# Output projection of a linear-attention block: a fifth Strassen unit, part of its input sums on GpSimd, and another order of the units

## The chip, the cores and the metric

The kernel runs on one core of one Trainium2 chip. A core has five engines that run side by side, each with its own instruction queue: TensorE (PE, matmuls; its weight loads appear as PEld), VectorE (DVE), ScalarE (ACT), GpSimd (POOL) and SyncE (SP), which here issues most DMAs. They wait for each other through semaphores. Matmuls write into PSUM, eight banks of 128 x 512 fp32 values; everything else lies in SBUF. The metric is the device time of one execution in microseconds.

## The reference

```python
def _A_ref(x, wqkv, wo):
    qkv = ... (x @ wqkv) split into q, k, v of 32 heads of 32
    phi = lambda t: jnp.where(t > 0, t + 1, jnp.exp(t)) + 1e-6
    pq, pk = phi(q), phi(k)
    kv = jnp.einsum("bhsd,bhse->bhde", pk, v)
    z = jnp.einsum("bhsd->bhd", pk)
    num = jnp.einsum("bhqd,bhde->bhqe", pq, kv)
    den = jnp.einsum("bhqd,bhd->bhq", pq, z)[..., None] + 1e-6
    return (num / den) as (S, D) @ wo

def _B_ref(x, w_gate, w_up, w_down):
    return (silu(x @ w_gate) * (x @ w_up)) @ w_down

xn = layernorm(x)
out = x + _A_ref(xn, wqkv, wo) * silu(_B_ref(xn, w_gate, w_up, w_down))
```

x has 2048 rows of 1024, the feed-forward width is 3584, inputs are bfloat16. The change touches the last product of `_A_ref`, (num / den) @ wo.

## The kernel before

The 2048 rows are four blocks (b = 0 to 3) of 512, each of four tiles (t) of 128 rows. The kernel has three stages.

Stage one computes K and V and sums kv and z over all rows. Stage two takes the blocks in turn. `emit_Q` (L178) computes the Q product of one of eight groups g in a PSUM bank, and `emit_phi` (L145) applies phi: with `act=True` three ScalarE passes and one VectorE pass, which is put off (`phi_late`); with `in_place=True` and `act=False` one ScalarE pass (Exp) and two VectorE passes (L157, L163). `emit_ND` (L725, "nd" below) makes numerator and denominator of one tile and divides on VectorE; `emit_OT` (L753) transposes the result by a DMA from the SP queue into oT, the left operand of the output projection. oT has two buffers, so block 3 writes the one that block 1 used. `emit_S` (L758) is the direct projection: for one tile and one half of the columns, eight matmuls and one scaled copy on ScalarE; a ScalarE-issued DMA then stores the tile to `s_dram`. Stage three is the feed-forward part, from L940 on, which starts from sums of the normalized input made by `emit_Ssum` (L696, four VectorE sums S1 to S4 of 128 x 2048).

The last tiles of the projection are done by Strassen units (`s_unit`, L785): two tiles t1 and t2 and both column halves form a 2 x 2 by 2 x 2 block product, which takes seven products of four matmuls where the direct way takes 32 matmuls. A unit works in these steps, each an entry of a dictionary:

- sums: four sums so1, so2, so3 and S4 of 128 x 512 from the two oT tiles (L801 to L804, VectorE). S4 is written over part of the oT tile.
- x: product into bank X; ScalarE copies X into bank Y (L814).
- w: product of so1 into W; ScalarE makes w1 from W (L821).
- y: product of so2 added onto Y; ScalarE copies Y into bank Z (L826) and makes s2 from Y (L827).
- x2: product added onto X; ScalarE writes a result quarter (L831).
- z: product of so3 added onto Z; VectorE adds w1 and writes a quarter (L835, a scalar_tensor_tensor, "STT" below).
- z2: product added onto Z; ScalarE writes a quarter (L840); SP stores the tile.
- w2: product of S4 added onto W; VectorE adds s2 and writes a quarter (L845); SP stores the other tile.

The right operands of w, y, z and z2 are four sums of wo (To_sb), made once by GpSimd (L780). The kernel before has four units, two for block 2 and two for block 3; blocks 0 and 1 are direct. All of TensorE, VectorE, ScalarE, GpSimd and SP's queue stand in program order here, so the order of calls is the order of execution on each engine. The five banks are fx0 to fx4. s2 and e_t of `emit_phi` share two buffers (tag e_t); w1 has two (tag r_t).

Beside this, `prep_step` (L352) prepares weights for stage three: a load, a ScalarE pass of squares (L288), a power of two, a VectorE scaling (L311), four GpSimd sums (L323 to L326) and a store. Some of it runs inside `nd_item` (L860). Stage three's first weight loads wait for the x product of the unit that holds tile 0 of block 3 (`first_gate`, marks[("S", 3, 0)]).

Of the kernel before, what the change touches and what calls it, by code (L numbers as in the profile page):

```python
# [10 lines left out]
ALU = mybir.AluOpType  # L11
# [10 lines left out]
def kernel(  # L22
# [155 lines left out]
    def emit_Q(b, g, act=None):  # L178
        pqT = pqT_of(b)
        btok = slice(b * TB, (b + 1) * TB)  # L180
        q_ps = ps2.tile([P, TB], FP32, name="q_ps", tag="B2")
        for dc in range(DC):
            nc.tensor.matmul(q_ps[:], lhsT=wq_sb[:, dc, g * P:(g + 1) * P], rhs=xn_ap(dc, btok),  # L183
                             start=(dc == 0), stop=(dc == DC - 1))
        emit_phi(phiw, q_ps[:], pqT[:, g, :], TB, in_place=True, act=b > 0 if act is None else act)
# [528 lines left out]
    with ExitStack() as p2:  # L714
# [43 lines left out]
        def emit_S(b, t, cc, bank=None):  # L758
            oT = oT_tiles[b]
            ttok = slice(t * P, (t + 1) * P)  # L760
            if (b, t) not in s_tiles:
                s_tiles[(b, t)] = work.tile([P, D], BF16, name="s_sb", tag="s_sb")
            s_sb = s_tiles[(b, t)]
            s_ps = bank or ps2.tile([P, CW], FP32, name="s_ps", tag="B2")
            for c in range(G):
                mm = nc.tensor.matmul(s_ps[:], lhsT=oT[:, c, ttok], rhs=wo_sb[:, c, cc * CW:(cc + 1) * CW],  # L766
                                      start=(c == 0), stop=(c == G - 1))
                marks.setdefault(("S", b, t), mm)
            nc.scalar.activation(out=s_sb[:, cc * CW:(cc + 1) * CW], in_=s_ps[:], func=ACT.Copy, scale=s_sc[:])
            if cc == NCC - 1:  # L770
                r0 = b * TB + t * P
                nc.scalar.dma_start(out=s_dram[r0:r0 + P, :], in_=s_tiles.pop((b, t))[:])
# [9 lines left out]
        fx = []  # L782
        unit_n = [0]

        def s_unit(b, u):  # L785
            n = unit_n[0]
            unit_n[0] += 1
            oT = oT_tiles[b]
            t1, t2 = u, u + 2
            k1, k2_ = slice(t1 * P, (t1 + 1) * P), slice(t2 * P, (t2 + 1) * P)  # L790
            a11, a12 = oT[:, 0:HG, k1], oT[:, HG:G, k1]
            a21, a22 = oT[:, 0:HG, k2_], oT[:, HG:G, k2_]
            b11, b21, b22 = wo_sb[:, 0:HG, 0:CW], wo_sb[:, HG:G, 0:CW], wo_sb[:, HG:G, CW:D]
            X, Y, Z, W = fx[n % 2], fx[1 - n % 2], fx[2], fx[3 + n % 2]
            so = wq_sb[:, TPB:DC, :].rearrange("p a b -> p (a b)")[:, (n % 2) * 2048:(n % 2) * 2048 + 3 * HG * P]
            so = so.bitcast(F16).rearrange("p (q k t) -> p q k t", q=3, k=HG)
            S4 = a21.bitcast(F16)
            sb = {}

            def sums():  # L800
                nc.vector.tensor_tensor(out=so[:, 0], in0=a21, in1=a22, op=ALU.add)  # L801
                nc.vector.tensor_tensor(out=so[:, 1], in0=so[:, 0], in1=a11, op=ALU.subtract)
                nc.vector.tensor_tensor(out=so[:, 2], in0=a11, in1=a21, op=ALU.subtract)
                nc.vector.tensor_tensor(out=S4, in0=a12, in1=so[:, 1], op=ALU.subtract)  # L804

            def mmk(out, a_, b_, first):
                for k in range(HG):
                    mm = nc.tensor.matmul(out[:], lhsT=a_[:, k, :], rhs=b_[:, k, :], start=first and k == 0,  # L808
                                          stop=k == HG - 1, skip_group_check=True)
                return mm  # L810

            def x():
                marks[("S", b, u)] = mmk(X, a11, b11, True)
                nc.scalar.copy(out=Y[:], in_=X[:])  # L814

            def w():
                for t in (t1, t2):
                    s_tiles[(b, t)] = work.tile([P, D], BF16, name="s_sb", tag="s_sb")
                mmk(W, so[:, 0], To[0], True)
                sb["w"] = phiw.tile([P, CW], FP32, name="w1", tag="r_t")  # L820
                nc.scalar.activation(out=sb["w"][:], in_=W[:], func=ACT.Copy, scale=s_sc[:])  # L821

            def y():
                mmk(Y, so[:, 1], To[1], False)
                s2 = sb["s2"] = phiw.tile([P, CW], FP32, name="s2", tag="e_t")
                nc.scalar.copy(out=Z[:], in_=Y[:])  # L826
                nc.scalar.activation(out=s2[:], in_=Y[:], func=ACT.Copy, scale=s_sc[:])  # L827

            def x2():
                mmk(X, a12, b21, False)  # L830
                nc.scalar.activation(out=s_tiles[(b, t1)][:, 0:CW], in_=X[:], func=ACT.Copy, scale=s_sc[:])  # L831

            def z():
                mmk(Z, so[:, 2], To[2], False)
                nc.vector.scalar_tensor_tensor(out=s_tiles[(b, t2)][:, CW:D], in0=Z[:], scalar=s_sc[:],  # L835
                                               in1=sb["w"][:], op0=ALU.mult, op1=ALU.add)

            def z2():
                mmk(Z, a22, To[3], False)
                nc.scalar.activation(out=s_tiles[(b, t2)][:, 0:CW], in_=Z[:], func=ACT.Copy, scale=s_sc[:])  # L840
                out_s(b, t2)

            def w2():
                mmk(W, S4, b22, False)
                nc.vector.scalar_tensor_tensor(out=s_tiles[(b, t1)][:, CW:D], in0=W[:], scalar=s_sc[:],  # L845
                                               in1=sb["s2"][:], op0=ALU.mult, op1=ALU.add)
                out_s(b, t1)
            return dict(sums=sums, x=x, w=w, y=y, x2=x2, z=z, z2=z2, w2=w2)

        def out_s(b, t):  # L850
            r0 = b * TB + t * P
            nc.sync.dma_start(out=s_dram[r0:r0 + P, :], in_=s_tiles.pop((b, t))[:])

        def q_item(b, g):
            return lambda: emit_Q(b, g)

        def s_item(b, t, cc):
            return lambda: emit_S(b, t, cc)
# [15 lines left out]
        def mix(a, b_):  # L874
            r = []
            for k in range(max(len(a), len(b_))):
                r += a[k:k + 1] + b_[k:k + 1]
            return r

        def sh(b, hf):  # L880
            return [s_item(b, t, cc) for t in (2 * hf, 2 * hf + 1) for cc in range(NCC)]

        def run(body, at, b, order=(0, 1, 2, 3)):
            for k, f in enumerate(body):
                f()
                if k in at:
                    nd_item(b, order[at.index(k)])()
                phi_flush()

        def qs(b):  # L890
            return [q_item(b, g) for g in range(G)]

        run(qs(1), (1, 3, 5, 7), 0)
        q = qs(2)
        run(q[:2] + mix(q[2:], sh(0, 0) + sh(0, 1)), (1, 4, 7, 10), 1)
        q = qs(3)
        run(q[:2] + mix(q[2:], sh(1, 0)), (1, 4, 7, 10), 2, (0, 2, 1, 3))
        nds = [nd_item(3, t) for t in (0, 2, 1, 3)]
        emit_S(1, 2, 0)
        emit_S(1, 2, 1)  # L900
        fx.extend([ps2.tile([P, CW], FP32, name="fx%d" % k, tag="B2") for k in range(5)])
        units = [s_unit(2, 0), s_unit(2, 1)]
        u = units[0]
        nds[0]()
        u["x"]()
        u["sums"]()
        emit_S(1, 3, 0, fx[4])
        nds[1]()
        emit_S(1, 3, 1, fx[2])
        u["w"]()  # L910
        units[1]["sums"]()
        u["y"]()
        u["x2"]()
        nds[2]()
        u["z"]()
        parts = []
        for n in range(1, 4):
            u, v = units[n - 1], units[n]
            for st in ('x w nd new -z2 sums y -w2 x2 z', 'x w new Ssum -z2 sums p y -w2 x2 z p', 'x w -z2 y p -w2 z x2 p z2 silu w2')[n - 1].split():
                if st == "nd":  # L920
                    nds[3]()
                elif st == "new":
                    units.append(s_unit(3, n - 1))
                elif st == "sums":
                    units[n + 1]["sums"]()
                elif st == "p":
                    parts.pop(0)()
                elif st == "silu":
                    nc.scalar.preload_act_table(ACT.Silu)
                elif st == "Ssum":  # L930
                    blk_es.close()
                    blk12_es.close()
                    sp = ctx.enter_context(tc.tile_pool(name="p3S", bufs=1, side="right", reuse_waits="tile"))
                    emit_Ssum(passes[0], parts)
                    stat_ps[0] = lambda: psa_tile("st_ps3")[0][:, 0, 511:512]
                    prep_flush()
                elif st[0] == "-":
                    u[st[1:]]()
                else:
                    v[st]()  # L940
    p2_man.close()
    p12.close()

# [987 lines left out]
```

## Time and profile before

| what | us |
|---|---|
| runs before | 750.99, 751.78, 752.26 (median 751.78) |
| the profiled execution, its own time | 751.34 |
| span from its first to its last instruction | 749.6 |
| DMA, mean rate | 259 GB/s |

Line 1 of the page has each engine's busy time, its share of the span and its number of instructions; part 4 has the chain of work that ended last. A row of the order of time has the start in us from the span's start, the length, the engine, the line, the operation, what it writes and reads, and how many instructions were merged; in brackets the idle time before it and what ended it. A row of merged matmuls lasts until the last one's modelled end, so the next row starts 0.16 us before the former ends when TensorE runs without a gap. The granted TensorE clock is 1.000 over the span. The units of stage two stand between 214.5 and 244.3 us:

```profile
L808 PE MATMUL fx<-wo_sb,oT x48: 377/379/380, 214.5 to 244.1; 128*128 128x512 bf16 x48
L814 ACT COPY fx<-fx x4: 570/570/570, 215.6 to 237.4; 128x512 f32<-128x512 f32 x4
L826 ACT COPY fx<-fx x4: 570/570/570, 221.2 to 240.0; 128x512 f32<-128x512 f32 x4
L827 ACT ACTIVATE s<-fx,s_sc x4: 692/692/692, 221.7 to 240.5; 128x512 f32<-128x512 f32 x4
```

### The profile page before, as it was taken

The page shows a single profiled execution, that of the slowest core. Times are in us where ns is not written, and L with a number is a line of the kernel's source. Part 1 is how long each engine was busy: PE and PEld are TensorE (multiplying, and loading weights), DVE is VectorE, ACT ScalarE, POOL GpSimd, SP SyncE. Part 2 cuts the span into 40 slices and gives each one's busy share as a digit, 9 for nine tenths or more (in the row PEclk, how much of TensorE's full clock was granted, in tenths as well). Part 3 has the DMA queues.
Part 4 walks back from the last instruction along what each step waited for, and adds up shares of the span by engine and source line. Part 5 has one row for each costly group of instructions (what it writes and reads, how often), then busy time and mean ns, then how long its engine had stood idle before and what let it go on. Part 6 is the DMA issues. An engine that isn't in the chain of part 4 may idle for free.

```text
span 749.6 us, 11280 instructions
## 1 busy us (share of the span) xinstructions
PE 741.9 (99%) x3962; PEld 370.8 (49%) x3962; DVE 590.6 (79%) x1046; ACT 385.6 (51%) x556; POOL 403.2 (54%) x435
## 2 busy tenths in 40 slices
PE   8999999999999999999999999999999999999997
PEld 3544444454454444444444444644444444467665
DVE  6577788887697688788889886587877767688897
ACT  5677866889965666667557511232222232322023
POOL 0111799998640255858586027310766676770076
PEclk9999999999999999999999999999999999999999
DMA  9957799869678668787889417998698889668854
GB/s 316 337 139 149 219 329 307 310 151 263 208 202 273 229 223 289 274 322 279 320 270 417 169 48 295 269 373 282 225 306 305 307 290 347 244 221 315 279 172 92
DMA packets 132425, 194.21 MB, mean 259 GB/s; under 512 B 36384, under 2 KB 106144, under 8 KB 122640
## 3 DMA queue, kind: packets, MB, share of 16 engines
q1 hardware_dynamic: 123600, 158.69, 65.3%
q0 software_dynamic: 7328, 32.31, 11.6%
q10 hardware_dynamic: 1440, 2.49, 1.0%
q8 instruction: 31, 0.51, 0.3%
q14 instruction: 26, 0.21, 0.1%
HBM read 122.68 MB, written 63.96 MB: 249 GB/s over the span
## 4 chain that ended last, share of the span: by engine, by line
PE 94%; DVE 3%; DMA 1%; ACT 1%; issue 1%; POOL 1%; DVEq 0%; ACTq 0%; POOLq 0%; SPq 0%
PE zw L958 25%; PE kv_ps L546 15%; PE xb L958 13%; PE q_ps L183 6%; PE dzw L1252 6%; PE yb L958 6%; PE dm L1533 5%; PE dm L1497 3%; PE fx L808 3%; PE s_ps L766 3%; PE dx L1252 2%; PE dy L1252 2%; PE dm L1252 1%; PE kvz L568 1%; PE nd L735 1%
## 5 line engine op out<-in xcount | busy, mean ns | idle before, releaser
L958 PEld LDWEIGHTS <-w_sb 128*128 128x128 f16 (+1 forms) x1568 | 152.0, 98 | 183.1 <-issue 0.5
L958 PE MATMUL xb<-xnT,w_sb 128*128 128x512 bf16 x448 | 115.0, 379 | 0.0
L546 PE MATMUL kv_ps<-wkv_sb,xnT 128*128 128x512 bf16 x512 | 113.8, 379 | 0.6 <-ACT xnT L535 0.4
L958 PE MATMUL zw<-xnT,w_sb 128*128 128x512 bf16 x448 | 105.9, 379 | 0.0
L958 PE MATMUL zw<-S,w_sb 128*128 128x512 f16 x448 | 105.8, 379 | 0.0
L323 POOL TENSOR_TENSOR w_sb<-w_sb 128x512 f16<-128x512 bf16 x42 | 50.7, 1206 | 99.9 <-DVE w_sb L311 51.2
L288 ACT ACTIVATE w_sb<-w_sb 128x2048 bf16<-128x2048 bf16 x42 | 79.9, 1902 | 3.5 <-DMA w_sb<-in_B_w_up_dram 2.4
L546 PEld LDWEIGHTS <-xnT 128*128 128x128 bf16 x512 | 48.3, 97 | 56.0 <-ACT xnT L535 0.8
L1139 POOL TENSOR_TENSOR w_sb<-w_sb 128x512 f16<-128x512 f16 (+3 forms) x48 | 50.0, 1063 | 28.5 <-DMA w_sb<-wd 27.5
L1034 ACT ACTIVATE sg<-cg 128x1024 bf16<-128x1024 f32 x28 | 29.6, 1057 | 57.6 <-DVE cg L1027 57.6
L183 PE MATMUL q_ps<-xnT,wq_sb 128*128 128x512 bf16 x256 | 58.4, 379 | 0.4 <-DVE pqT L151 0.4
L958 PE MATMUL yb<-S,w_sb 128*128 128x512 f16 x224 | 57.5, 379 | 0.0
L1027 DVE SCALAR_TENSOR_TENSOR cg<-zw,rc_all,s 128x1024 f32<-128x1024 f32 x28 | 35.9, 1283 | 25.3 <-PE zw L958 12.8
L986 DVE SCALAR_TENSOR_TENSOR s<-yb,rc_all,s 128x512 f32<-128x512 f32 x42 | 31.4, 749 | 27.9 <-ACT s L985 27.9
L324 POOL TENSOR_TENSOR w_sb<-w_sb 128x512 f16<-128x512 bf16 x42 | 50.7, 1207 | 3.3
L1230 POOL DMA_DIRECT2D out_dram<-io x16 | 8.7, 544 | 80.7 <-DVE io L1229 80.5
L326 POOL TENSOR_TENSOR w_sb<-w_sb 128x512 f16<-128x512 bf16 x42 | 50.3, 1197 | 0.0
L325 POOL TENSOR_TENSOR w_sb<-w_sb 128x512 f16<-128x512 bf16 x42 | 49.8, 1185 | 0.0
L985 ACT ACTIVATE s<-xb,rcl 128x512 f32<-128x512 f32 x14 | 9.6, 687 | 65.0 <-PE xb L958 65.0
L985 ACT ACTIVATE s<-xb,rc_all 128x512 f32<-128x512 f32 x42 | 28.4, 675 | 21.9 <-issue 12.7
L311 DVE TENSOR_SCALAR w_sb<-w_sb,cs_all 128x2048 bf16<-128x2048 bf16 x35 | 36.2, 1035 | 3.5 <-DVE cs_all L301 0.8
L183 PEld LDWEIGHTS <-wq_sb 128*128 128x128 bf16 x256 | 24.4, 97 | 28.1 <-issue 0.6
(232 smaller groups left out, 1364.4 us busy)
## 6 DMA issues: line engine op xcount, KB each, us to landing
w_sb<-pk_g SPq DMA_DIRECT2D x27, 1024.0 KB, 6.4
pk_g<-w_sb SPq DMA_DIRECT2D x14, 1024.0 KB, 5.0
w_sb<-pk_u SPq DMA_DIRECT2D x14, 1024.0 KB, 8.5
pk_u<-w_sb POOLq DMA_DIRECT2D x13, 1024.0 KB, 5.5
w_sb<-l SPq DMA_DIRECT2D x12, 896.0 KB, 5.6
l<-w_sb POOLq DMA_DIRECT2D x9, 896.0 KB, 7.7
w_sb<-in_B_w_gate_dram SPq DMA_DIRECT2D x14, 512.0 KB, 6.6
w_sb<-in_B_w_down_dram SPq DMA_DIRECT2D x28, 256.0 KB, 4.7
```

The costliest lines, as they stand in the source:

```text
L183: nc.tensor.matmul(q_ps[:], lhsT=wq_sb[:, dc, g * P:(g + 1) * P], rhs=xn_ap(dc, btok), start=(dc == 0), stop=(dc == DC - 1))
L288: nc.scalar.activation(out=junk, in_=raw_view(key, t), func=ACT.Square, accum_out=asum[:])
L323: nc.gpsimd.tensor_tensor(out=T1, in0=b12, in1=b11, op=ALU.subtract)
L324: nc.gpsimd.tensor_tensor(out=T2, in0=b22, in1=T1, op=ALU.subtract)
L325: nc.gpsimd.tensor_tensor(out=T3, in0=b22, in1=b12, op=ALU.subtract)
L326: nc.gpsimd.tensor_tensor(out=T4, in0=b21, in1=T2, op=ALU.subtract)
L546: mm = nc.tensor.matmul(kv_ps[:], lhsT=xn_ap(dc, tok), rhs=wkv_sb[:, dc, c * CW:(c + 1) * CW], start=(dc == 0), stop=(dc == DC - 1))
L958: mm = nc.tensor.matmul(out, lhsT=lhs(k), rhs=rhs(k), start=(first and k == 0), stop=(k == HK - 1), skip_group_check=True)
L985: nc.scalar.activation(out=s1[:], in_=x_[:], func=ACT.Copy, scale=rc)
L1139: nc.gpsimd.tensor_tensor(out=b(o_), in0=b(a_), in1=b(b_), op=ALU.subtract)
L1252: nc.tensor.matmul(out, lhsT=lhs, rhs=rhs, start=first, stop=lastk, skip_group_check=True)
L1533: nc.tensor.matmul(out, lhsT=lhs, rhs=w[:, j], start=i == 1 and j == 0, stop=j == NQ - 1, skip_group_check=True)
```

## The change

Block 1's tiles 2 and 3 are a fifth unit (unit 0, n = 0) in place of four calls of `emit_S`. Units are numbered 0 to 4: (1; 2, 3), (2; 0, 2), (2; 1, 3), (3; 0, 2), (3; 1, 3). The sums of units 0, 2 and 3 are made by GpSimd, those of units 1 and 4 by VectorE, and unit 1's are emitted in two pairs (`sum_a`, `sum_b`). Unit 0's are emitted before the Q products of block 3, into phi's r_t buffers; its w1 copy comes after its y product.

The copy of Y into Z is gone: the z and z2 products add onto Y itself, after s2 has read it. A unit then uses three banks at a time, and five banks serve units that overlap by one more step. The order of steps is one list, `UNIT_STAGE`, in which a name ends in its unit's number; nd takes the next tile of block 3 (0, 2, 1, 3), p the next sum of `emit_Ssum`. The last Q product (block 3, group 7) uses the form of phi with two VectorE passes.

```diff
-        def s_unit(b, u):
+        def s_unit(b, t1, t2, early=False, eng=nc.vector):
...
-            X, Y, Z, W = fx[n % 2], fx[1 - n % 2], fx[2], fx[3 + n % 2]
+            if early:
+                se = [phiw.tile([P, 2, HG, P], F16, name="se%d" % k, tag="r_t") for k in range(2)]
+                so1, so2, so3 = se[0][:, 0], se[0][:, 1], se[1][:, 0]
...
+            X, Y, W = lambda: fx[(0, 3, 1)[n % 3]], lambda: fx[(1, 0, 3)[n % 3]], lambda: fx[2 + n % 2 * 2]
...
+            def sum_a():
+                eng.tensor_tensor(out=so1, in0=a21, in1=a22, op=ALU.add)
+                eng.tensor_tensor(out=so2, in0=so1, in1=a11, op=ALU.subtract)
+
+            def sum_b():
+                eng.tensor_tensor(out=so3, in0=a11, in1=a21, op=ALU.subtract)
+                eng.tensor_tensor(out=S4, in0=a12, in1=so2, op=ALU.subtract)
...
             def y():
-                mmk(Y, so[:, 1], To[1], False)
+                mmk(Y(), so2, To[1], False)
                 s2 = sb["s2"] = phiw.tile([P, CW], FP32, name="s2", tag="e_t")
-                nc.scalar.copy(out=Z[:], in_=Y[:])
-                nc.scalar.activation(out=s2[:], in_=Y[:], func=ACT.Copy, scale=s_sc[:])
+                nc.scalar.activation(out=s2[:], in_=Y()[:], func=ACT.Copy, scale=s_sc[:])
+                if early:
+                    w_copy()
...
             def z():
-                mmk(Z, so[:, 2], To[2], False)
+                mmk(Y(), so3, To[2], False)
...
         def q_item(b, g):
-            return lambda: emit_Q(b, g)
+            return lambda: emit_Q(b, g, act=(b, g) != (NB - 1, G - 1))
...
+        units = [s_unit(1, 2, 3, early=True, eng=nc.gpsimd)]
+        units[0]["sums"]()
         q = qs(3)
         run(q[:2] + mix(q[2:], sh(1, 0)), (1, 4, 7, 10), 2, (0, 2, 1, 3))
         nds = [nd_item(3, t) for t in (0, 2, 1, 3)]
-        emit_S(1, 2, 0)
-        emit_S(1, 2, 1)
         fx.extend([ps2.tile([P, CW], FP32, name="fx%d" % k, tag="B2") for k in range(5)])
-        units = [s_unit(2, 0), s_unit(2, 1)]
-        u = units[0]
-        nds[0]()
-        u["x"]()
-        u["sums"]()
-        emit_S(1, 3, 0, fx[4])
-        nds[1]()
-        emit_S(1, 3, 1, fx[2])
-        u["w"]()
-        units[1]["sums"]()
-        u["y"]()
-        u["x2"]()
-        nds[2]()
-        u["z"]()
+        units += [s_unit(2, 0, 2), s_unit(2, 1, 3, eng=nc.gpsimd)]
+        units[2]["sums"]()
         parts = []
-        for n in range(1, 4):
-            u, v = units[n - 1], units[n]
-            for st in ('x w nd new -z2 sums y -w2 x2 z', 'x w new Ssum -z2 sums p y -w2 x2 z p', 'x w -z2 y p -w2 z x2 p z2 silu w2')[n - 1].split():
+        n_new = 0
+        UNIT_STAGE = """x0 w0 y0 x20 z0 nd x1 z20 sum_a1 w20 sum_b1 x21 w1 y1 x2 z1 nd x22 z21 w21 w2 nd new sums3 y2
+            x3 z2 nd new Ssum x23 z22 w22 p w3 y3 sums4 x4 z3 p w4 z23 y4 p w23 z4 x24 p z24 silu w24"""
+        for st in UNIT_STAGE.split():
...
+                    units.append(s_unit(3, n_new, n_new + 2, eng=nc.vector if n_new else nc.gpsimd))
```

In the list x2, z2 and w2 of unit n read x2n, z2n and w2n (x20 is unit 0's x2), while x2, y2, z2 and w2 without a further digit are unit 2's x, y, z and w.

More of the change, by code (lines that the diff above doesn't have):

```diff
@@ L788, in s_unit @@
             oT = oT_tiles[b]
-            t1, t2 = u, u + 2
             k1, k2_ = slice(t1 * P, (t1 + 1) * P), slice(t2 * P, (t2 + 1) * P)
@@ L793, in s_unit @@
             b11, b21, b22 = wo_sb[:, 0:HG, 0:CW], wo_sb[:, HG:G, 0:CW], wo_sb[:, HG:G, CW:D]
-            X, Y, Z, W = fx[n % 2], fx[1 - n % 2], fx[2], fx[3 + n % 2]
-            so = wq_sb[:, TPB:DC, :].rearrange("p a b -> p (a b)")[:, (n % 2) * 2048:(n % 2) * 2048 + 3 * HG * P]
-            so = so.bitcast(F16).rearrange("p (q k t) -> p q k t", q=3, k=HG)
+            if early:
+                se = [phiw.tile([P, 2, HG, P], F16, name="se%d" % k, tag="r_t") for k in range(2)]
+                so1, so2, so3 = se[0][:, 0], se[0][:, 1], se[1][:, 0]
+            else:
+                so = wq_sb[:, TPB:DC, :].rearrange("p a b -> p (a b)")[:, (n % 2) * 2048:(n % 2) * 2048 + 3 * HG * P]
+                so = so.bitcast(F16).rearrange("p (q k t) -> p q k t", q=3, k=HG)
+                so1, so2, so3 = so[:, 0], so[:, 1], so[:, 2]
+            X, Y, W = lambda: fx[(0, 3, 1)[n % 3]], lambda: fx[(1, 0, 3)[n % 3]], lambda: fx[2 + n % 2 * 2]
             S4 = a21.bitcast(F16)
             sb = {}
+            def sum_a():
[4 more added lines that the diff above has]
+                eng.tensor_tensor(out=S4, in0=a12, in1=so2, op=ALU.subtract)
             def sums():
[L801 to L804, printed above, removed]
+                sum_a()
+                sum_b()
             def mmk(out, a_, b_, first):
@@ L812, in x, with w @@
             def x():
-                marks[("S", b, u)] = mmk(X, a11, b11, True)
-                nc.scalar.copy(out=Y[:], in_=X[:])
-            def w():
+                marks[("S", b, t1)] = mmk(X(), a11, b11, True)
+                nc.scalar.copy(out=Y()[:], in_=X()[:])
                 for t in (t1, t2):
                     s_tiles[(b, t)] = work.tile([P, D], BF16, name="s_sb", tag="s_sb")
-                mmk(W, so[:, 0], To[0], True)
+            def w():
+                mmk(W(), so1, To[0], True)
+                if not early:
+                    w_copy()
@@ L820, in w, with w_copy @@
+            def w_copy():
                 sb["w"] = phiw.tile([P, CW], FP32, name="w1", tag="r_t")
-                nc.scalar.activation(out=sb["w"][:], in_=W[:], func=ACT.Copy, scale=s_sc[:])
+                nc.scalar.activation(out=sb["w"][:], in_=W()[:], func=ACT.Copy, scale=s_sc[:])
             def y():
-                mmk(Y, so[:, 1], To[1], False)
+                mmk(Y(), so2, To[1], False)
                 s2 = sb["s2"] = phiw.tile([P, CW], FP32, name="s2", tag="e_t")
-                nc.scalar.copy(out=Z[:], in_=Y[:])
@@ L827, in y @@
-                nc.scalar.activation(out=s2[:], in_=Y[:], func=ACT.Copy, scale=s_sc[:])
+                nc.scalar.activation(out=s2[:], in_=Y()[:], func=ACT.Copy, scale=s_sc[:])
+                if early:
+                    w_copy()
             def x2():
-                mmk(X, a12, b21, False)
-                nc.scalar.activation(out=s_tiles[(b, t1)][:, 0:CW], in_=X[:], func=ACT.Copy, scale=s_sc[:])
+                mmk(X(), a12, b21, False)
+                nc.scalar.activation(out=s_tiles[(b, t1)][:, 0:CW], in_=X()[:], func=ACT.Copy, scale=s_sc[:])
@@ L833, in z @@
             def z():
-                mmk(Z, so[:, 2], To[2], False)
-                nc.vector.scalar_tensor_tensor(out=s_tiles[(b, t2)][:, CW:D], in0=Z[:], scalar=s_sc[:],
+                mmk(Y(), so3, To[2], False)
+                nc.vector.scalar_tensor_tensor(out=s_tiles[(b, t2)][:, CW:D], in0=Y()[:], scalar=s_sc[:],
                                                in1=sb["w"][:], op0=ALU.mult, op1=ALU.add)
             def z2():
-                mmk(Z, a22, To[3], False)
-                nc.scalar.activation(out=s_tiles[(b, t2)][:, 0:CW], in_=Z[:], func=ACT.Copy, scale=s_sc[:])
+                mmk(Y(), a22, To[3], False)
@@ L841, in z2 @@
+                nc.scalar.activation(out=s_tiles[(b, t2)][:, 0:CW], in_=Y()[:], func=ACT.Copy, scale=s_sc[:])
                 out_s(b, t2)
             def w2():
-                mmk(W, S4, b22, False)
-                nc.vector.scalar_tensor_tensor(out=s_tiles[(b, t1)][:, CW:D], in0=W[:], scalar=s_sc[:],
+                mmk(W(), S4, b22, False)
+                nc.vector.scalar_tensor_tensor(out=s_tiles[(b, t1)][:, CW:D], in0=W()[:], scalar=s_sc[:],
                                                in1=sb["s2"][:], op0=ALU.mult, op1=ALU.add)
@@ L847, in w2 @@
                 out_s(b, t1)
-            return dict(sums=sums, x=x, w=w, y=y, x2=x2, z=z, z2=z2, w2=w2)
+            return dict(sums=sums, sum_a=sum_a, sum_b=sum_b, x=x, w=w, y=y, x2=x2, z=z, z2=z2, w2=w2)
         def out_s(b, t):
@@ L898 @@
         nds = [nd_item(3, t) for t in (0, 2, 1, 3)]
-        emit_S(1, 2, 0)
-        emit_S(1, 2, 1)
         fx.extend([ps2.tile([P, CW], FP32, name="fx%d" % k, tag="B2") for k in range(5)])
-        units = [s_unit(2, 0), s_unit(2, 1)]
-        u = units[0]
-        nds[0]()
-        u["x"]()
-        u["sums"]()
-        emit_S(1, 3, 0, fx[4])
-        nds[1]()
-        emit_S(1, 3, 1, fx[2])
-        u["w"]()
-        units[1]["sums"]()
-        u["y"]()
-        u["x2"]()
-        nds[2]()
-        u["z"]()
-        parts = []
-        for n in range(1, 4):
-            u, v = units[n - 1], units[n]
-            for st in ('x w nd new -z2 sums y -w2 x2 z', 'x w new Ssum -z2 sums p y -w2 x2 z p', 'x w -z2 y p -w2 z x2 p z2 silu w2')[n - 1].split():
+        units += [s_unit(2, 0, 2), s_unit(2, 1, 3, eng=nc.gpsimd)]
+        units[2]["sums"]()
+        parts = []
+        n_new = 0
+        UNIT_STAGE = """x0 w0 y0 x20 z0 nd x1 z20 sum_a1 w20 sum_b1 x21 w1 y1 x2 z1 nd x22 z21 w21 w2 nd new sums3 y2
+            x3 z2 nd new Ssum x23 z22 w22 p w3 y3 sums4 x4 z3 p w4 z23 y4 p w23 z4 x24 p z24 silu w24"""
+        for st in UNIT_STAGE.split():
+                n = int(st[-1]) if st[-1].isdigit() else 0
                 if st == "nd":
-                    nds[3]()
+                    nds.pop(0)()
                 elif st == "new":
-                    units.append(s_unit(3, n - 1))
-                elif st == "sums":
-                    units[n + 1]["sums"]()
+                    units.append(s_unit(3, n_new, n_new + 2, eng=nc.vector if n_new else nc.gpsimd))
+                    n_new += 1
+                elif st == "silu":
+                    nc.scalar.preload_act_table(ACT.Silu)
                 elif st == "p":
                     parts.pop(0)()
-                elif st == "silu":
-                    nc.scalar.preload_act_table(ACT.Silu)
                 elif st == "Ssum":
@@ L936 @@
                     prep_flush()
-                elif st[0] == "-":
-                    u[st[1:]]()
                 else:
-                    v[st]()
+                    units[n][st[:-1]]()
     p2_man.close()
```

## The prediction

> **What bounds the kernel now.** I read the busy shares first, then the chain that ended last, then, because the change touches only the end of the output projection, the order of time there, engine by engine.
>
> ```profile
> PE 741.9 (99%) x3962; PEld 370.8 (49%) x3962; DVE 590.6 (79%) x1046; ACT 385.6 (51%) x556; POOL 403.2 (54%) x435
> ...
> PE 94%; DVE 3%; DMA 1%; ACT 1%; issue 1%; POOL 1%; DVEq 0%; ACTq 0%; POOLq 0%; SPq 0%
> ```
>
> TensorE is busy 99% of the span and is 94% of the chain. So a matmul removed is worth its issue interval, and any wait that reaches TensorE is paid in full. TensorE in order of time (start, length):
>
> ```profile
> 210.61 3.62 PE L766 MATMUL s_ps<-wo_sb,oT 128*128 128x512 bf16 x16
> 214.06 0.63 PE L735 MATMUL nd<-KVZ,pqT 128*128 128x132 bf16 x8
> 214.53 1.02 PE L808 MATMUL fx<-wo_sb,oT 128*128 128x512 bf16 x4
> ...
> 225.20 0.64 PE L735 MATMUL nd<-KVZ,pqT 128*128 128x132 bf16 x8
> 225.94 1.02 PE L808 MATMUL fx<-To_sb,oT 128*128 128x512 f16 x4
> ...
> 242.55 1.02 PE L808 MATMUL fx<-To_sb,oT 128*128 128x512 f16 x4
> ...
> 244.28 1.03 PE L958 MATMUL yb<-S,w_sb 128*128 128x512 f16 x4
> ```
>
> Sixteen matmuls issue in 214.06 - 210.61 = 3.45 us, so a product of four takes 0.8625, and an nd 214.53 - 214.06 = 0.47. From the last Q product's end (210.61) to the next stage (244.28) are 33.67 us. Filled without a gap, 36 products and four nds would be 31.05 + 1.88 = 32.93: only 0.74 us is waiting, near 225.2, 225.9 and 242.5. The stage is already tight.
>
> **The change part by part.**
>
> **Products.** The 32 direct matmuls for tiles 2 and 3 of block 1 become a unit of 28: 35 products and four nds, 35 x 0.8625 + 1.88 = 32.07. If nothing waited the stage would gain 33.67 - 32.07 = 1.60 us (0.86 from four matmuls, 0.74 from waits). That is the ceiling of the whole change.
>
> The new waits come from laying the new order out from 210.61, on VectorE, ScalarE, GpSimd and the SP queue beside it:
>
> ```profile
> 211.77 1.38 DVE L311 TENSOR_SCALAR w_sb<-w_sb,cs_all 128x2048 bf16<-128x2048 bf16 x1
> 213.07 1.27 DVE L151 SCALAR_TENSOR_TENSOR pqT<-e_t,q_ps 128x512 bf16<-128x512 f32 x2
> ...
> 216.80 1.38 DVE L801 TENSOR_TENSOR wq_sb<-oT 128x512 f16<-128x512 bf16 x1
> ...
> 231.18 0.41 DVE L801 TENSOR_TENSOR wq_sb<-oT 128x512 f16<-128x512 bf16 x1
> ```
>
> ```profile
> 216.75 1.15 POOL L326 TENSOR_TENSOR w_sb<-w_sb 128x512 f16<-128x512 bf16 x1
> ```
>
> Read them together: the same sum takes VectorE 0.41 us with GpSimd idle, but 1.38 while L326 runs, ending 0.28 after it (217.90 to 218.18).
>
> **Unit 0 and the last Q product.** x0, w0, y0, x20 stand at 210.61, 211.47, 212.34, 213.20. z0 now adds onto the bank that the copy s2 reads, so it waits for s2. s2 writes an e_t buffer that the first L151 above frees at 213.07 + 0.69 = 213.76; s2 is 213.80 to 214.49 (0.69, the L827 row), z0 at 214.54 and not 214.06: +0.48. I take it whole, since that L151 and the L311 before it do not move. The last Q product's two VectorE passes (0.69 each, rows L157 and L151) follow that L151: 213.67 to 215.09, 0.75 later than before. nd 0, at 215.40, covers this; without 0.31 of cover TensorE would wait. ScalarE loses two passes there and four bank copies (0.57 each); it was idle between products, so this is worth nothing.
>
> **Early sums.** Unit 0's four GpSimd sums (4.5 us, as the four To_sb sums at L780) fall into GpSimd's idle 6.17 us before 195.79, after block 1's last transpose has landed. Free; a transpose 1.6 us later would push the next weight sums, whose weights are used tens of us later.
>
> **Unit 1 on VectorE against unit 2 on GpSimd.** z0's STT runs 215.6 to 216.35, nd 0's chain (2.15 us, from 214.73 to 216.88 in the old trace) to 218.42. Then sum_a1's two sums. GpSimd finishes L326 at 217.90 and goes straight into unit 2's sums. By the 1.38 row, the first sum ends 0.28 after GpSimd's first (219.05), at 219.33; the second after GpSimd's second (220.48), at 220.76. x1, z20, w20, x21, w1 fill TensorE to 220.19, so y1 starts at 220.81: +0.62. Bounds: nothing if GpSimd leaves gaps; and, by the row below, all four GpSimd sums in one (to 222.4, so1 at 222.7, w1 at 222.73 and not 219.32): +3.41. I take 0.62, the row with the same instruction.
>
> ```profile
> 163.61 4.50 POOL L780 TENSOR_TENSOR To_sb<-wo_sb,To_sb 128x512 f16<-128x512 bf16 x4
> ...
> 164.43 4.23 DVE L311 TENSOR_SCALAR w_sb<-w_sb,cs_all 128x2048 bf16<-128x2048 bf16 x1
> ```
>
> The Trainium skill (SBUF — State Buffer, "Who interferes with whom") says that a VectorE instruction with two SBUF inputs and a GpSimd one that reads SBUF exclude each other, and that the loser blocks until the holder's single instruction is done; it advises to plan which of the two is off the critical path, which speaks against this split. The 1.38 row agrees; the 4.23 row, over four GpSimd instructions, goes beyond it. By the rule the wait is the 0.62 above.
>
> z1 waits 0.07 for its s2. The two s_dram stores that leave ScalarE's queue for SP's (0.32 each) stand between transposes that come later anyway: free.
>
> **The tail.** nds 1, 2 and 3 move late: nd 1 at 223.46, nd 2 at 227.38, nd 3 at 230.44, where the old kernel had its last at 225.20. After nd 3 come seven products (x23, z22, w22, w3, y3, x4, z3), then w4 at 236.95 and z23 at 237.81. Against that stands a chain: z2's STT ends at 231.39, nd 3's VectorE work (2.15) at 233.46, the transpose issues at 233.50, lands, and only then unit 4's four sums run on VectorE. z3's STT is queued behind them, and z23 waits for that STT.
>
> ```profile
> L756 SPq DMA_TRANSPOSE oT<-wq_sb x4: 1232/1234/1297, 219.5 to 228.1; - x4
> ...
> DMA to landing us min/median/max: 3.0/4.3/6.3
> ```
>
> A transpose takes 3.0 to 6.3 us over the sixteen. The sums take 1.67 (231.18 to 232.85 before, GpSimd idle), the STT 0.75, handovers 0.05: z23 = landing + 2.44. At the median, 237.80 + 2.44 = 240.24: +2.43, of which w4 already pays 1.4 for its first sum. At 3.0: +1.13. At 6.3: +4.43. I take the median: the 1 MB weight load, gated by unit 3's x (x3 ends 229.74), is now queued on SP just ahead of transpose 3, and the two transposes issued within 0.7 us of a 1 MB store (200.85, 206.59) were the 6.3 and a 5.3, while alone (194.43, 228.06) they took 3.0 and 3.1. SP waits there for x3 only until 229.8, and transpose 3's data is ready at 230.2, so the queue order itself costs nothing.
>
> Unit 3's GpSimd sums (from about 231, 4.5 us and 1.2 more by S1 on VectorE beside them) precede w3 to z3 in step. At the end z4 waits 0.07 for s2 and z24 0.14 for an STT, much as 242.55 does now. The stage sums S2 to S4 end before the next stage needs them.
>
> **The sum.** 32.07 + 0.48 + 0.62 + 0.07 + 2.43 + 0.07 + 0.14 = 35.88, less 33.67 = +2.2 us. What follows is TensorE bound and only shifts. The profiled execution took 751.34 (span 749.6 and 1.74 around it) and would take 753.6; the median of the runs is 0.44 higher, so 754.0.
>
> **The rivals.**
>
> (a) Both costs are at their floors: transpose 3.0 and GpSimd no hindrance, 2.21 - 1.30 - 0.62 = +0.3, up to +1.5 with a little of each: 752.1 to 753.3. For it: two of the last four landed in 3.0 to 3.1. Against: neither had a load just ahead.
>
> (b) VectorE is kept out for the whole GpSimd chain at unit 1: +2.21 + 2.79 = +5.0, 756.8. For it the 4.23 row; against it the 1.38 row and most L311 rows, which waited for one instruction.
>
> (c) The other side, not slower: the tail wait at z23 does not exist. It decides at one point: the last transpose must land by 235.37, 1.9 us after its issue. Then the sum is 2.21 - 2.43 = -0.2: 751.6; with the port conflict also gone -0.8, and with every wait gone the ceiling, -1.6: 750.2. For it: the removed products are certain. Against: none of sixteen landed under 3.0.
>
> (d) The waits are right but the next stage takes them back, because it had been waiting itself: 751.8. Against: its matmuls follow each other from 244.28 on, with one gap of 0.15 near 310.
>
> **How the numbers follow.** Forecast 0.53, its own range 753.0 to 756.2; (a) 0.22; (b) 0.10; (c) 0.12; (d) 0.03. A difference of 0.2% (1.5 us) is about what the measurement can tell from none. Faster by more is half of (c) at most and what I have not seen: 0.08. Same: the rest of (c), (d), most of (a), the forecast's lower edge: 0.30. Slower: 0.62. The range 751.2 to 757.0 holds (a), the forecast, (d) and most of (b), and leaves out the ceiling of (c) and both dear ends together (758.8).
>
> **What would show it.** Right: gaps on TensorE ahead of z0 (about 0.5), y1 (about 0.6) and around w4 and z23 (together about 2.4), the last transpose landing near 237.8, VectorE's sums of unit 1 at 1 to 1.4 us each, the next stage beginning near 246.5. Wrong: z23 following w4 without a gap, or a next stage that begins before 244.3.

## The result, and the profile after

| | before | after |
|---|---|---|
| median of the runs, us | 751.53 (6 runs) | 754.66 (6 runs) |
| ratio, 95% interval | | 1.0042 (1.0029 to 1.0055) |
| span of the profiled execution, us | 749.6 | 753.0 |
| last Q product's end to the next stage's first matmul, us | 33.67 | 36.61 |
| TensorE's waits in that stretch, us | 0.7 | 4.5 |

The change removes four matmuls and makes the kernel slower by 3.1 us. Busy time first, the page's part 1 of the changed kernel:

```profile
PE 742.2 (99%) x3958; PEld 371.1 (49%) x3958; DVE 592.7 (79%) x1041; ACT 383.2 (51%) x551; POOL 418.3 (56%) x447
```

The count of matmuls fell from 3962 to 3958 and ScalarE lost 2.4 us, while GpSimd gained 15. The shares over the span hardly show the loss; the stage does. TensorE in order of time (start, length, engine, line, operation; in brackets the idle time before and who ended it):

```profile
210.72 1.03 PE L818 MATMUL fx<-wo_sb,oT 128*128 128x512 bf16 x4
...
214.69 1.02 PE L818 MATMUL fx<-To_sb,se 128*128 128x512 f16 x4 [0.35 <-ACT s L840]
...
220.75 1.04 PE L818 MATMUL fx<-To_sb,wq_sb 128*128 128x512 f16 x4 [0.25 <-DVE wq_sb L806]
...
230.47 0.63 PE L735 MATMUL nd<-KVZ,pqT 128*128 128x132 bf16 x8
...
233.53 1.89 PE L818 MATMUL fx<-To_sb,wq_sb 128*128 128x512 f16 x8
237.70 1.04 PE L818 MATMUL fx<-wo_sb,oT 128*128 128x512 bf16 x4 [2.28 <-DMA oT<-wq_sb]
238.57 1.89 PE L818 MATMUL fx<-To_sb,wq_sb 128*128 128x512 f16 x8
241.03 1.02 PE L818 MATMUL fx<-To_sb,oT 128*128 128x512 f16 x4 [0.57 <-DVE s_sb L850]
...
247.33 1.03 PE L960 MATMUL yb<-S,w_sb 128*128 128x512 f16 x4
```

The idle time in brackets counts from the former matmul's modelled end; counted from the time at which the next could have been issued, each wait is 0.16 longer. So z0 (214.69) waits 0.51, y1 (220.75) 0.41, x4 (237.70) 2.44 and z23 (241.03) 0.73; four waits of 0.08 to 0.20 make up the rest of 4.5. Three of the four large ones stand where the prediction put them. The largest, x4, is one it did not name: x4 is unit 4's first product, its left operand is tile 1 of block 3, and that comes by transpose 3, the third of block 3's four (behind nd 2; the nds count from 0). The SP queue of the changed kernel in order of time shows it (the two transposes merged into one row):

```profile
229.73 0.32 SPq L265 DMA_DIRECT2D w_sb<-pk_g  x1
230.19 5.53 SPq L756 DMA_TRANSPOSE oT<-wq_sb  x2
```

The view of line L756 in a window around 230.19, so of transpose 3 alone, has its time from issue to landing:

```profile
DMA to landing us min/median/max: 7.5/7.5/7.5
```

The 1 MB weight load is issued 0.46 us ahead of transpose 3; the load lands at 235.80, the transpose at 237.65 and the last one (issued 233.56) at 238.48, after 4.92 us:

```profile
DMA to landing us min/median/max: 4.9/4.9/4.9
```

VectorE then runs unit 4's sums, and z3's STT (L850) behind them:

```profile
218.55 0.85 DVE L805 TENSOR_TENSOR wq_sb<-oT 128x512 f16<-128x512 bf16 x1
219.43 1.26 DVE L806 TENSOR_TENSOR wq_sb<-wq_sb,oT 128x512 f16<-128x512 f16 x1
...
221.27 0.71 DVE L809 TENSOR_TENSOR wq_sb<-oT 128x512 f16<-128x512 bf16 x1
222.01 1.26 DVE L810 TENSOR_TENSOR oT<-oT,wq_sb 128x512 f16<-128x512 bf16 x1
...
238.58 0.43 DVE L805 TENSOR_TENSOR wq_sb<-oT 128x512 f16<-128x512 bf16 x1 [2.91 <-DMA oT<-wq_sb]
...
240.23 0.74 DVE L850 SCALAR_TENSOR_TENSOR s_sb<-fx,s_sc,w 128x512 bf16<-128x512 f32 x1
```

The first four rows are unit 1's sums beside GpSimd's, 0.71 to 1.26 us each; unit 4's, with GpSimd idle, begin at 0.43. GpSimd's four sums of unit 2 in the same stretch:

```profile
217.96 1.15 POOL L805 TENSOR_TENSOR wq_sb<-oT 128x512 f16<-128x512 bf16 x1
219.19 1.22 POOL L806 TENSOR_TENSOR wq_sb<-wq_sb,oT 128x512 f16<-128x512 f16 x1
220.37 1.33 POOL L809 TENSOR_TENSOR wq_sb<-oT 128x512 f16<-128x512 bf16 x1
221.78 1.21 POOL L810 TENSOR_TENSOR oT<-oT,wq_sb 128x512 f16<-128x512 bf16 x1
```

Each VectorE sum ends 0.28 or 0.29 us after one of GpSimd's (the first at 219.40, after 219.11): it got in behind a single one, and none waited for the whole chain.

### The profile page after: what moved, and what is told of

It reads as the page before. It is cut to its first block, busy times and chain, and to the rows that moved or that the text cites. A ratio compares the mean times of both kernels' runs of the same rounds, so it can differ in the third digit from the quotient of the medians.

```text
span 753.0 us, 11276 instructions
## 1 busy us (share of the span) xinstructions
PE 742.2 (99%) x3958; PEld 371.1 (49%) x3958; DVE 592.7 (79%) x1041; ACT 383.2 (51%) x551; POOL 418.3 (56%) x447
## 4 chain that ended last, share of the span: by engine, by line
PE 67%; DVE 0%; issue 0%; DVEq 0%
PE zw L960 26%; PE xb L960 13%; PE yb L960 6%; PE dzw L1254 6%; PE dm L1535 6%; PE dm L1499 4%; PE dy L1254 2%; PE dx L1254 2%; PE dm L1254 1%; PE fx L818 1%; PE dm L1647 1%; DVE g L1230 0%; DVE io L1231 0%; DVE l2c L1487 0%; PE yb L292 0%
```

## The experiments

"Stage" is always the time from the last Q product's end to the next stage's first matmul: 33.67 us before the change, 36.61 after it.

### The load gate moved

```diff
-                first_gate[0] = marks[("S", NB - 1, 0)]
+                first_gate[0] = marks[("S", NB - 1, 1)]
```

> Stage three's first weight loads wait for the x product of unit 4 instead of unit 3's, so the 1 MB load is queued behind the last two transposes and not ahead of transpose 3. Nothing else changes. Theory (the load delays the transposes): transpose 3 lands in 3 to 4 us instead of 7.5, x4 (2.4 us late in the changed kernel) starts without a wait, what is left at the tail is the last transpose plus the sums and the STT queued behind it, about 1.1 to 1.9 us; the time falls by 1.2 to 2.2 us against the changed kernel, to about 752.5 to 753.5. Rival (the late place of the nd products alone delays the tail, the load is no part of it): transposes land as late as before, no change. Second rival (the next stage pays for its later loads): the tail's wait goes but the time stays.

Measured: 752.74 us, ratio to the kernel before 1.0016 (1.0006 to 1.0025); stage 34.74. SP's queue of this run:

```profile
230.16 4.61 SPq L756 DMA_TRANSPOSE oT<-wq_sb  x2
...
237.83 0.57 SPq L265 DMA_DIRECT2D w_sb<-pk_g  x1
```

And transpose 3 alone, from issue to landing:

```profile
DMA to landing us min/median/max: 3.8/3.8/3.8
```

Issued at the same time (230.16 against 230.19), transpose 3 now lands after 3.84 us and not 7.46, the last one after 3.04 and not 4.92:

```profile
DMA to landing us min/median/max: 3.0/3.0/3.0
```

TensorE at the tail:

```profile
235.22 1.03 PE L818 MATMUL fx<-wo_sb,oT 128*128 128x512 bf16 x4
236.16 2.03 PE L818 MATMUL fx<-To_sb,wq_sb 128*128 128x512 f16 x8
239.12 1.02 PE L818 MATMUL fx<-To_sb,oT 128*128 128x512 f16 x4 [0.93 <-DVE s_sb L850]
```

x4 (235.22) follows without a wait, and z23 (239.12) waits 1.09. z23 starts 2.54 us after the last transpose's landing (236.58), in the changed kernel 2.55 after it (238.48), so the stage gained what the last transpose gained. The load delayed the transposes: 1.9 us of the 3. The rivals fall: neither did the transposes stay late, nor did the next stage pay for the later load beyond the scatter of its length (506.0 us, against 505.2 to 506.0 over all the profiles).

### z3 ahead of unit 4's sums

```diff
-            w3 y3 sums4 x4 z3 p w4
+            w3 y3 x4 z3 sums4 p w4
```

> Unit 4's four sums are emitted after unit 3's z step instead of before x4, so that z3's STT no longer stands behind them in VectorE's queue. Theory (two separate waits at the tail: the transposes, 2.4 us at x4, and VectorE's queue, 0.7 at z23): the wait at z23 goes, w4 waits a little for its first sum, sum of the tail's waits 2.4 to 2.8 instead of 3.2; the time falls by 0.4 to 0.8 us. Rival (z23 follows the transposes whatever VectorE's order): no change in the tail's sum.

Measured: 755.19 us, ratio 1.0051 (1.0034 to 1.0068); stage 37.18, 0.6 longer. The theory was wrong in this form, and so was the rival: the wait at z23 goes, but w4's is twice as long. TensorE:

```profile
238.09 1.03 PE L818 MATMUL fx<-To_sb,wq_sb 128*128 128x512 f16 x4
240.35 1.04 PE L818 MATMUL fx<-To_sb,wq_sb 128*128 128x512 f16 x4 [1.23 <-DVE wq_sb L805]
```

z3 (238.09) is itself behind x4 and so late; the sums now wait for its STT, and w4 (240.35) waits 1.40 for the first of them. VectorE's queue is a cause only together with what stands on TensorE between the sums and their users; turning the two round only changes who waits.

### Unit 2's sums on VectorE

```diff
-        units += [s_unit(2, 0, 2), s_unit(2, 1, 3, eng=nc.gpsimd)]
-        units[2]["sums"]()
+        units += [s_unit(2, 0, 2), s_unit(2, 1, 3)]
...
-            w20 sum_b1 x21
+            w20 sum_b1 sums2 x21
```

> Unit 2's four sums go from GpSimd to VectorE, right after unit 1's. Theory (unit 1's sums on VectorE wait for GpSimd's): unit 1's sums take 0.42 us each instead of 0.7 to 1.3, the wait before y1 (0.42) goes, and VectorE still has unit 2's sums ready before w2; the stage ends 0.2 to 0.5 us sooner. Rival (VectorE is full there, and what GpSimd took off comes back): the wait reappears at z1, nd 1 or z21, no gain or a loss of up to 1 us.

Measured: 753.10 us, ratio 1.0019 (1.0010 to 1.0029); stage 35.07. VectorE's order of time:

```profile
218.46 0.42 DVE L805 TENSOR_TENSOR wq_sb<-oT 128x512 f16<-128x512 bf16 x1
218.91 0.42 DVE L806 TENSOR_TENSOR wq_sb<-wq_sb,oT 128x512 f16<-128x512 f16 x1
```

The sums take 0.42 each, and the wait before y1 is gone and comes back nowhere: the theory. VectorE does all eight sums of units 1 and 2 by 222.4, where in the changed kernel it needed until 223.3 for four. The stage gained 1.5 and not 0.4, because both late transposes were issued 0.5 us earlier and were also quicker: the last one landed after 3.83 us and not 4.92, transpose 3 after 6.29 and not 7.46 (x4 waited 1.27 and not 2.44). Behind the same load transpose 3 took 7.3 to 7.5 us in all four kernels with unit 2's sums on GpSimd, and 6.3 to 6.4 in both with them on VectorE. The view of the DMA queues has a candidate for the difference. Over transpose 3 of the changed kernel, from issue to landing, it lists two packets of a second queue, of kind "instruction", beside the queue of these transfers (packets, MB, share of the 16 DMA engines):

```profile
q1 hardware_dynamic: 2017, 1.58, 95.7%
q14 instruction: 2, 0.02, 0.9%
```

All six kernels with unit 2's sums on GpSimd have two such packets in that flight, the four with them on VectorE none. It is the same with no load ahead: 3.84 us with the packets (gate moved, also with y4 ahead), 3.04 and 3.06 without (all four together). No run moved the packets alone, so that they are the cause is not shown.

### The last Q product with three ScalarE passes

```diff
-            return lambda: emit_Q(b, g, act=(b, g) != (NB - 1, G - 1))
+            return lambda: emit_Q(b, g, act=None)
```

> The last Q product gets back the form with three ScalarE passes. Theory (z0's wait of 0.5 is that of s2 for its buffer, and ScalarE would be late with the copy of X into Y if it had the two passes more): y0 waits about 0.7 to 0.9 instead, z0 hardly, sum of the waits before nd 0 the same within 0.3; the time is that of the changed kernel within 0.5. Rival (the two VectorE passes hold up unit 0): the waits before nd 0 fall by 0.4 or more.

Measured: 755.27 us, ratio 1.0045 (1.0030 to 1.0060); stage 36.48.

TensorE:

```profile
212.98 1.02 PE L818 MATMUL fx<-To_sb,se 128*128 128x512 f16 x4 [0.57 <-ACT fx L824]
```

y0 (212.98) waits 0.74 for the copy of X into Y, z0 then 0.08 and not 0.51: the theory. Together that is 0.3 more than before, and y1's wait falls by as much, from 0.41 to 0.12. The two-pass form moves a wait from y0 to z0 and is worth nothing by itself here.

### y4 ahead of z23, with the load gate moved

```diff
-            p w4 z23 y4 p w23 z4
+            p w4 y4 z23 p w23 z4
```

> The later load gate (as in the run with the gate moved) and, in the list, unit 4's y before unit 3's z2 (w4 y4 z23 in place of w4 z23 y4), so that one product more lies between VectorE's sums of unit 4 with z3's STT behind them and the product that waits for that STT. Theory (what was left at the tail is VectorE's queue: last transpose, four sums, STT, and then z23): the wait of 1.1 before z23 falls to 0.3 or less, the stage takes 33.8 to 34.1 us instead of 34.7, the time falls by 0.6 to 1.0 us against the run with the gate alone. Rival (the wait follows the sums themselves: y4 waits for the second one): the wait moves to y4 and the time stays.

Measured: 751.69 us, ratio 1.0002 (0.9993 to 1.0011); stage 33.79. z23's wait is 0.23 and not 1.09, y4 does not wait: the theory, and 1.0 us. z23 still starts 2.54 us after the last landing (236.45); one product more now stands in that time. With two edits, the gate and two steps exchanged, the changed kernel takes the time of the one before.

### Unit 0's s2 in another buffer

```diff
-                sb["w"] = phiw.tile([P, CW], FP32, name="w1", tag="r_t")
+                sb["w"] = phiw.tile([P, CW], FP32, name="w1", tag="e_t" if early else "r_t")
...
-                s2 = sb["s2"] = phiw.tile([P, CW], FP32, name="s2", tag="e_t")
+                s2 = sb["s2"] = phiw.tile([P, CW], FP32, name="s2", tag="r_t" if early else "e_t")
```

> The changed kernel, but unit 0's s2 takes a buffer of its sums (tag r_t) and its w1 the e_t buffer, so s2 no longer waits for the STT of a Q product. Theory (z0's wait of 0.5 is this buffer): z0 starts without a wait. But VectorE's chain (nd 0, then unit 1's sums beside GpSimd's) keeps its place, so the 0.5 comes back as a wait of w1 or y1, whose sum grows from 0.4 to about 0.9: time the same within 0.3. Rival (the gain stays): the stage is 0.4 to 0.5 us shorter.

Measured: 754.14 us, ratio 1.0039 (1.0025 to 1.0054); stage 36.59.

TensorE:

```profile
214.34 1.02 PE L818 MATMUL fx<-To_sb,se 128*128 128x512 f16 x4
...
219.48 1.04 PE L818 MATMUL fx<-To_sb,wq_sb 128*128 128x512 f16 x4 [0.20 <-DVE wq_sb L805]
220.77 1.04 PE L818 MATMUL fx<-To_sb,wq_sb 128*128 128x512 f16 x4 [0.26 <-DVE wq_sb L806]
```

z0's wait shrinks from 0.51 to 0.14 (the theory had it gone), and w1 (219.48), which had none, now waits 0.37 for VectorE, y1 0.42 as before. The 0.37 came back in full: between z0 and y1 VectorE's chain sets the time, beside GpSimd's sums.

### All four together

The gate, unit 2's sums on VectorE, y4 ahead of z23 and the two buffers; run twice.

> All four repairs together: the load gate on unit 4's x, unit 2's sums on VectorE, y4 before z23, and the swapped buffers of unit 0's s2 and w1. Theory (four separate waits, of about 1.9, 0.4, 0.85 and 0.5 us, that add): the stage takes 33.0 to 33.4 us, 0.3 to 0.7 less than before the change (33.67) and 3.2 to 3.6 less than after it; the time is 751.0 to 751.6, at or a little under the kernel before. Rival (the waits share VectorE and come back elsewhere): the stage takes 33.9 us or more.

> The kernel with all four repairs once more, for a narrower interval against the kernel before. Theory: stage 32.9 to 33.2 us, 0.5 to 0.7 less than before, so a ratio of 0.9991 to 0.9995. Rival (the next stage gives it back): ratio 0.9998 or more.

Measured: 750.99 us, ratio 0.9994 (0.9985 to 1.0002); again 751.11 us, ratio 0.9995 (0.9986 to 1.0004). The stage is 32.94 and 32.96, 0.7 us under the kernel before, with 0.9 of waits left in the first. Now that VectorE is not held by GpSimd, the buffers' 0.4 us stays: z0 waits 0.14, and neither w1 nor y1 waits. Both ratios lie under one and both intervals reach just past it: the stage's gain of 0.7 us is shown by the profiles, that of the whole kernel is at the edge of what these runs tell.

### Three of the four, with the load ahead again

> Three of the four repairs, with the load gate back on unit 3's x as in the changed kernel. Theory (the load ahead of transpose 3 is a cost of its own): transpose 3 lands in 6 to 7.5 us instead of 3.1, x4 waits about 2 us, the stage takes 34.6 to 35.4 us instead of 32.9, the time grows by 1.6 to 2.4 us against the run with all four. Rival (the repairs overlap, and y4's place hides the transposes): the stage takes 33.6 us or less.

Measured: 751.79 us, ratio 1.0008 (0.9998 to 1.0017); stage 33.99. Between the two expectations: transpose 3 lands after 6.44 us and x4 waits 1.42, 0.6 less than expected. TensorE:

```profile
235.77 1.04 PE L818 MATMUL fx<-wo_sb,oT 128*128 128x512 bf16 x4 [1.26 <-DMA oT<-wq_sb]
236.65 2.75 PE L818 MATMUL fx<-To_sb,wq_sb 128*128 128x512 f16 x12
```

The load is a cost of its own, 1.0 us here and 1.9 in the changed kernel. After the wait at x4 the twelve matmuls of z3, w4 and y4 run through, because TensorE is now late enough: the last transpose lands at 236.63, the first sum ends at 237.09, and w4 needs it at 237.51. z23 follows without a wait too, 2.61 us after that landing. The waits at the tail stand in one line, so what one repair is worth depends on the others.

## Why the prediction was right, and where its sizes were off

What bounds the kernel: right. Every wait in the stage reached the end, and the next stage gave nothing back (rival d): it began 3.05 us later, and the span grew by 3.4.

The ceiling of 1.60 us: right as a count. 36.61 less 4.53 of waits is 32.08, the 32.07 of the sum. No run reached it; the best stage, 32.94, has 0.9 of waits left.

The sum, term by term, forecast and measured:

| wait | forecast | measured |
|---|---|---|
| z0, for s2's buffer | 0.48 | 0.51 |
| y1, for unit 1's sums beside GpSimd | 0.62 | 0.41 |
| tail: x4, w4 and z23 | 2.43 | 3.17 |
| small ones | 0.28 | 0.44 |
| all | 3.81 | 4.53 |

z0 was confirmed by the run with the buffers exchanged: 0.37 of the 0.51 went. y1 was confirmed by the run with unit 2's sums on VectorE; it was smaller, because the second sum ended at 220.69, 0.2 us sooner than laid out (220.76, in a stage that began 0.11 later). The rule cited from the Trainium skill (SBUF — State Buffer, "Who interferes with whom"), that a loser waits for one instruction, held here: 0.71 to 1.26 us for each VectorE sum beside GpSimd's, where 0.42 is its own, and no wait of 4 us as in rival (b). The forecast of 1 to 1.4 us each was met by two of the four sums.

The tail is the term that was mis-sized, by 0.74. Its chain was right: the last transpose lands, VectorE makes four sums and z3's STT, and z23 starts. It does so 2.55 us after the landing, where the prediction has 2.44 (its three terms, 1.67, 0.75 and 0.05, add up to 2.47). With the steps in this order and unit 4's sums ahead of z3's STT, every profile has 2.49 to 2.55. What was too small is the landing: 4.92 us after the issue and not the median of 4.3. With the gate moved it took 3.04, and the stage became 1.9 us shorter: the load ahead, which the prediction gave only as a reason for the median, is what made the last transpose late.

What the prediction left out is transpose 3. It put the whole wait at w4 and z23, but w4 does not wait, and TensorE meets most of it at x4, three products earlier, because transpose 3 took 7.46 us, outside the range of 3.0 to 6.3. "The queue order itself costs nothing" was right for the issue (230.19, as laid out) and wrong for the landing: the rows with 5.3 and 6.3 us behind a 1 MB store were not read as transpose 3's own time. With 6.3 there, x4 would already have been forecast to wait over a second. By these rows x4's 2.44 us adds nothing by itself in the changed kernel: had transpose 3 alone come in time, z23 would have waited 3.17 for the last one. That it comes so near the 2.43 forecast for w4 and z23 is chance. The old trace also had transposes of 5.75 and 4.50 us (219.50 and 221.52) with no 1 MB transfer just ahead on SP's queue, which the prediction does not mention; so a 1 MB transfer ahead is not the only thing that goes with a long transpose.

The part on VectorE's queue, that z23 waits for an STT behind four sums, is right too: 1.09 us with the load out of the way, 0.23 when y4 comes ahead.

The early sums of unit 0 were free, as said: GpSimd ran them from 191.25 to 195.98, its next weight sums began 0.9 us later than before, and no wait on TensorE follows there. The last Q product's new form cost nothing and gained nothing, as said; the run that undid it shows that it trades y0's wait for z0's.

The median of 754.66 lies in the forecast's own range, 753.0 to 756.2. Against the forecast of 2.2 us the medians moved by 3.1: 0.7 of the difference is in the table, the tail above all. The profiled spans moved by 3.4, of which 2.94 lie in the stage, 0.11 before it and 0.34 after it; the time after it varies from 505.2 to 506.0 us over the profiles of all these kernels, whose later stages do the same work, so no cause was sought.

## What to carry to other kernels

On an engine that is 99% busy, removed instructions pay only if the new order leaves every chain between two of its products as much room as before: here four matmuls (0.86 us) were bought with the last three transposes issued 5.0 to 5.5 us later (226.5, 230.2 and 233.6 against 221.5, 225.2 and 228.1), which took away all their cover. Lay out each operand's arrival, not only the last one's: here the last one set the tail's length, but in the run with three repairs TensorE waited for the earlier one, transpose 3, alone. Price a transfer that is issued right behind a large one by such a row, not by the median. When waits share an engine, repair them together or measure the pairs: exchanging the two buffers gained nothing alone, and its 0.4 us stayed beside the other repairs.

## What the hardware showed that was not expected

A transpose issued 0.46 us behind a 1 MB load took 7.46 us, and 3.84 with that load moved behind it; in the kernels with the other three repairs it took 6.44 with the load ahead and 3.04 to 3.06 without. In the changed kernel it landed 1.85 us after the load, although its own data were ready when it was issued: on one queue the small transfer did not get past the large one. And two engines' sums that met took turns, instruction by instruction (VectorE 0.71 to 1.26 us, GpSimd 1.15 to 1.33): both were slowed, VectorE 1.7 to 3 times, GpSimd by 16% at most.
